# Queries and keys of chunks 0 and 1 as seven-product pairs, and the down stage of chunk 1 behind four gate/up tiles

## The chip, the cores and the metric

The kernel runs on one core of one Trainium2 chip. The metric is the device time of one execution in microseconds (us), median of several runs. The *granted clock* is the share of its full clock that TensorE was given. The span, from the first to the last instruction in the profile, is about 1.8 us shorter than the time. PE is TensorE, PEld its weight loads, DVE is VectorE, ACT is ScalarE, POOL is GpSimd, SP is SyncE, which only issues transfers here.

## The reference

```python
def reference(A_x, A_wqkv, A_wo, B_x, B_w_gate, B_w_up, B_w_down, gate_w):
    # x: 1 x 2048 x 1024 in bf16; 32 heads of 32; Df = 3584
    g = sigmoid((x * gate_w).sum(-1, keepdims=True))
    # a: local attention. Row s sees rows s, s-2, ..., s-14 (8 of them)
    qkv = (x @ wqkv).reshape(B, S, 3, H, Dh)
    logits = sum over Dh of q[s] * k[s - 2w], scaled, w = 0..7, masked below row 0
    a = (softmax(logits) weighted sum of v) @ wo
    # b: feed-forward on the same x
    b = (gelu(x @ w_gate) * (x @ w_up)) @ w_down
    return g * a + (1 - g) * b
```

(Shortened; the sums are written out in words.)

## The kernel before

The 2,048 rows are worked on in four chunks of 512. TensorE does the matrix products. VectorE does the attention: it multiplies queries by shifted keys, adds up, and later multiplies the weights by shifted values; each of these instructions covers 128 x 2,048 elements. Between the two steps the sums are turned over by transposing copies that SyncE issues, and the softmax runs on VectorE and ScalarE.

Many products are done two chunks at a time with seven products of half size in place of eight (Strassen's scheme in Winograd's form). That needs *forms*, sums and differences of the weights and of x, which VectorE makes ahead of the products, and afterwards additions, also on VectorE, from PSUM, the memory in whose banks the products land. Before the change, queries and keys of chunks 0 and 1 were computed plainly; the values, the second half's projections, gate/up and down were pairs already.

A list scheduler inside the program decides the order in which instructions are put down on each engine. It runs when the program is built, from its own estimates. On the chip the order is fixed: an engine whose next instruction must wait, waits, whatever stands behind it (6.11 us in an example below).

```python
    def main():                      # the order of TensorE's work (cut)
        # ... all 32 transposes of chunk 0's rows ...
        yield from qkv_outer(0)      # queries of chunk 0, plainly
        yield from qkv(0, 1)         # keys of chunk 0, plainly
        yield from gate(0)
        yield from qkv_pair(0, [2])  # values of chunks 0 and 1 as a pair
        yield from gate_sum(0)
        yield from qkv(1, 0)         # queries and keys of chunk 1, plainly
        yield from qkv(1, 1)
        yield from gate(1)
        yield from halo(1)
        for sup in range(NSUP):
            c0 = 2 * sup
            more = sup + 1 < NSUP
            parts = down(c0)
            yield from ffn(sup, parts, [gate_sum(1)] if sup == 0 else [])
            yield from parts[2]
            if more:
                yield from halo(c0 + 2)
                yield from gate(c0 + 2)
                yield from gate(c0 + 3)
                yield from qkv_pair(c0 + 2)      # "the second stage" below
                # ...
            for part in down(c0 + 1):            # down stage of chunk 1
                yield from part

    def gate(c):                     # (cut)
        i, free = bank_take()        # a PSUM bank
        # ... eight small matmuls into the bank ...
        zt = work.tile([P, SC], F32, tag="u2", bufs=2, name="zt")   # shares its two buffers with the u2 copies
        e = dve(0.63, lambda: nc.vector.transpose(out=zt[:], in_=banks[i][:]), [o])
        yield e
        bank_give(i, e)              # the bank is free when VectorE has read it
        e = dve(0.1, lambda: nc.vector.tensor_copy(out=zq[:], in_=...zt...), [e])
```

## Time and profile before

| | before |
|---|---|
| time, median of 3 runs | 725.7 us (725.52 to 726.15) |
| first gate/up product | 88.11 us |
| gates 2 and 3 begin | 312.65 us |
| second query/key/value stage ends | 387.26 us |
| last matmul ends | 720.08 us |

The prediction shows how busy the engines are. One stage that it does not cut out is needed later. This is its row in the table by stage (stretch, length, then busy time and count of PE, PEld, DVE, ACT, POOL, the granted clock, DMA share, GB/s), for the gates and projections of chunks 2 and 3:

```profile
312.65:387.26 74.61, 73.74 (x363) 44.38 (x369) 66.66 (x123) 37.58 (x66) 0.54 (x1) 1.00 0.39 115
```

The stage is 74.61 us long and PE is busy for 73.74 of them; DVE has 66.66 us of work and so 8 us of room.

### The profile page before, as it was taken

The numbers are of one execution on the slowest core, as the hardware profiler recorded it, in microseconds if no ns is written. First come the engines' busy times: TensorE is split into PE (matmuls) and PEld (weight loads), VectorE is DVE, ScalarE is ACT, GpSimd is POOL, SyncE is SP. The second block draws the span as 40 slices with busy tenths as digits, with TensorE's granted clock in tenths as the row PEclk, the third lists the DMA queues.
The fourth block names the chain that finished last, engine by engine and source line by source line (L and its number), as shares of the span: only waits on it lengthen the run. The fifth ranks groups of instructions, "written<-read, shape, count | busy, mean of one in ns | idle before, by whom it ended". The sixth has DMA issues, their size and how long they took to land.

```text
span 723.8 us, 9915 instructions
## 1 busy us (share of the span) xinstructions
PE 713.6 (99%) x3314; PEld 351.1 (49%) x3381; DVE 598.5 (83%) x898; ACT 315.3 (44%) x535; POOL 71.8 (10%) x128
## 2 busy tenths in 40 slices
PE   8999999999999999999999999999999999999997
PEld 5666644444444444455665444444444444444443
DVE  1799999999999899799599976999999995794200
ACT  2353465557655532035552114567558557110110
POOL 1000433343121100100000000000000000001000
PEclk9999999999999999999999999999999999999999
DMA  9944799989989979945239999786566657999992
GB/s 313 236 149 103 222 354 318 334 256 349 267 218 193 274 239 299 344 143 146 58 97 300 362 324 309 236 186 177 157 178 159 177 157 178 313 326 331 327 304 99
DMA packets 180931, 172.12 MB, mean 238 GB/s; under 512 B 56464, under 2 KB 137360, under 8 KB 180880
## 3 DMA queue, kind: packets, MB, share of 16 engines
q1 hardware_dynamic: 172048, 143.69, 68.5%
q0 software_dynamic: 8544, 27.27, 10.7%
q8 instruction: 26, 0.43, 0.2%
q10 hardware_dynamic: 288, 0.52, 0.2%
q14 instruction: 25, 0.20, 0.1%
HBM read 129.50 MB, written 28.31 MB: 218 GB/s over the span
## 4 chain that ended last, share of the span: by engine, by line
PE 83%; DVE 8%; DMA 4%; issue 4%; POOL 1%; ACT 0%; DVEq 0%; POOLq 0%; ACTq 0%
PE ps L995 35%; PE ps L1159 28%; PE ps L628 12%; PE ps L496 8%; DMA fforms<-ring 1%; DVE ring L457 1%; DVE ring L576 1%; DVE hT L1058 1%; DMA ring<-in_B_w_down_dram 1%; DMA ring<-in_A_wqkv_dram 1%; DMA hT<-in_A_wo_dram 1%; DMA hT<-in_B_w_down_dram 1%; DVE hT L1120 1%; DVE hT L1039 1%; DVE hT L433 0%
## 5 line engine op out<-in xcount | busy, mean ns | idle before, releaser
L995 PEld LDWEIGHTS <-ring 128*128 128x128 bf16 x1568 | 153.2, 98 | 185.8 <-issue 1.6
L995 PE MATMUL ps<-lend,ring 128*128 128x512 bf16 x877 | 210.5, 379 | 1.3 <-ACT m L1049 0.4
L995 PE MATMUL ps<-tf,ring 128*128 128x512 bf16 x659 | 162.6, 379 | 0.7
L1159 PE MATMUL ps<-ring,hT 128*128 128x512 bf16 x696 | 159.7, 379 | 0.6
L1159 PEld LDWEIGHTS <-hT 128*128 128x128 bf16 x708 | 69.2, 98 | 83.3
L945 DVE TENSOR_TENSOR xbuf<-xbuf,lend 128x2048 bf16<-128x2048 bf16 x64 | 77.4, 1215 | 7.5 <-DMA xbuf<-xbuf 7.5
L798 DVE TENSOR_TENSOR xbuf<-qo,lend 128x2048 bf16<-128x2048 bf16 x64 | 76.7, 1216 | 0.1
L804 DVE TENSOR_TENSOR xbuf<-xbuf 128x2048 bf16<-128x2048 bf16 x56 | 68.2, 1217 | 0.3
L628 PEld LDWEIGHTS <-ring 128*128 128x128 bf16 x384 | 49.3, 129 | 34.4 <-DVE lend L481 0.9
L1024 ACT COPY ps<-ps 128x512 f32<-128x512 f32 x56 | 32.0, 571 | 55.6 <-PE ps L995 55.5
L1067 ACT ACTIVATE gl<-ps 128x512 bf16<-128x512 f32 x56 | 33.5, 598 | 49.6 <-PE ps L995 48.5
L1194 ACT ACTIVATE ost<-ps,omg 128x512 bf16<-128x512 f32 x16 | 11.0, 688 | 100.6 <-PE ps L1159 81.9
L1186 POOL DMA_DIRECT2D out_dram<-ost x24 | 13.0, 540 | 411.0 <-ACT ost L1194 319.1
L1159 PE MATMUL ps<-ring,qo 128*128 128x512 bf16 x187 | 48.5, 379 | 0.2
L466 POOL DMA_DIRECT2D fforms<-ring x56 | 30.6, 546 | 175.3 <-DVE ring L457 166.1
L628 PE MATMUL ps<-lend,ring 128*128 128x512 bf16 x203 | 47.0, 380 | 0.7 <-DVE lend L481 0.5
L1039 DVE TENSOR_TENSOR hT<-hT,gl 128x1024 bf16<-128x1024 bf16 x56 | 38.3, 683 | 11.3 <-ACT hT L1036 11.3
L953 DVE TENSOR_TENSOR xbuf<-xbuf 128x1024 bf16<-128x1024 bf16 x64 | 42.0, 683 | 0.4
L1079 DVE TENSOR_TENSOR u<-ps,u 128x512 f32<-128x512 f32 x56 | 38.3, 684 | 4.6 <-PE ps L995 3.2
L628 PE MATMUL ps<-tf,ring 128*128 128x512 bf16 x173 | 40.1, 379 | 0.2
L1058 DVE TENSOR_TENSOR hT<-ps,m 128x512 bf16<-128x512 f32 x56 | 38.2, 683 | 1.5 <-PE ps L995 1.4
L1075 ACT COPY u<-ps 128x512 f32<-128x512 f32 x56 | 32.9, 587 | 15.1 <-PE ps L995 15.1
(110 smaller groups left out, 697.1 us busy)
## 6 DMA issues: line engine op xcount, KB each, us to landing
ring<-dforms SPq DMA_DIRECT2D x112, 256.0 KB, 5.3
ring<-in_B_w_down_dram SPq DMA_DIRECT2D x84, 256.0 KB, 4.6
ring<-in_B_w_gate_dram SPq DMA_DIRECT2D x56, 256.0 KB, 4.8
fforms<-ring POOLq DMA_DIRECT2D x56, 256.0 KB, 5.3
ring<-fforms SPq DMA_DIRECT2D x56, 256.0 KB, 4.0
ring<-in_B_w_up_dram SPq DMA_DIRECT2D x42, 256.0 KB, 4.7
ring<-in_A_wqkv_dram SPq DMA_DIRECT2D x32, 256.0 KB, 5.4
ring<-oforms SPq DMA_DIRECT2D x32, 256.0 KB, 5.7
```

Of the source, the lines that this page charges most:

```text
L496: nc.tensor.matmul(banks[bk][:], lhsT=lhsT, rhs=xT(c, kt), start=(kt == 0), stop=(kt == KT - 1))
L628: nc.tensor.matmul(banks[bk][:], lhsT=lhsT, rhs=rhs[:, kt, :], start=(start and kt == 0), stop=(kt == KH - 1), skip_group_check=True)
L798: V(out=w3(box[t]), in0=q_b, in1=k_w, op=ALU.mult)
L804: V(out=w3(box[0]), in0=w3(box[0]), in1=w3(box[t]), op=ALU.add)
L945: return dve(tt(n), taking(("p", t), lambda: V(out=w3(box["p", t]), in0=w3(box["ab"]), in1=v_w, op=ALU.mult)), [("qkv", c, 2, t), abo] + ( ...
L953: V(out=s4(t)[:, t % 2], in0=w3(box["p", t])[:, 0:4], in1=w3(box["p", t])[:, 4:8], op=ALU.add)
L995: nc.tensor.matmul(banks[bk][:], lhsT=wv[:, k, fl * P:(fl + 1) * P], rhs=rhs[:, k, :], start=(start and k == 0), stop=(k == KH - 1), skip_ ...
L1039: yield dve(tt(2 * SC), lambda f=f: nc.vector.tensor_tensor(out=hrow[:, f, :], in0=hrow[:, f, :], in1=gl[f][:], op=ALU.mult), [e, ev[f, "g ...
L1058: ev[f, "up2"] = dve(tt(SC, True), lambda f=f: nc.vector.tensor_tensor(out=hs(f, 1), in0=v3(banks[Bk[f]][:]), in1=v3(m5[f][:]), op=ALU.add ...
L1067: nc.scalar.activation(out=gl[f][:, SC:2 * SC], in_=banks[A[f]][:], func=ACT.Gelu_apprx_tanh)
L1079: e = dve(tt(SC, True), lambda f=f: nc.vector.tensor_tensor(out=u2[f][:], in0=banks[Dk[f]][:], in1=u2[f][:], op=ALU.add), [o, ev[f, "u2"]])
L1159: nc.tensor.matmul(banks[bk][:], lhsT=l, rhs=wv[:, i, :], start=(start and k == 0), stop=(q == last and i == 1), skip_group_check=True)
```

## The change

The intent: 32 matmuls fewer. Queries and keys of chunks 0 and 1 become pairs, like the values. The first of the seven products needs chunk 0 alone, so it is put at the front while chunk 1 is still on its way. Chunk 1's attention now starts later, so its down stage goes behind the first four gate/up tiles of the second half; that in turn needs chunk 3's queries, keys and values to be parked in DRAM for a while. Double-width forms, fewer and wider window sums, and new constants of the scheduler come with it.

```diff
     def main():
-        # 32 transposes, then
-        yield from qkv_outer(0)
-        yield from qkv(0, 1)
-        yield from gate(0)
+        yield from turn_rows()           # the first 16 transposes
+        yield from qkv_pair(0, [0])      # first_pair: chunk 0's products, 16 transposes, gates 0 and 1, the rest
+        yield from qkv_pair(0, [1])
+        yield from gate_sum(0)
+        yield from gate_sum(1)
         yield from qkv_pair(0, [2])
-        yield from gate_sum(0)
-        yield from qkv(1, 0)
-        yield from qkv(1, 1)
-        yield from gate(1)
         yield from halo(1)
...
+        yield from qkv_pair(2)
+        parts = down(1)
+        yield from ffn(1, 0, NE, parts)  # NE = 4: four gate/up tiles, then chunk 1's down stage
+        yield from parts[2]
+        parts = down(2)
+        yield from ffn(1, NE, FT, parts)
...
+    def park(which):                     # chunk 3's projections wait in DRAM
+        return Op("POOL", ..., lambda: nc.gpsimd.dma_start(out=parked[which]..., in_=hrow[:, r:r + NT, 0:SC]), ...)
...
-    w.run([(0.0, main()), (0.0, loads()), (0.0, late_x()), (0.88, wforms()), ..., (1.43, qkv_forms()), (1.3, preps()), (0.13, attention()), (0.36, scores())])
+    w.run([(0.0, main()), (0.0, loads()), (0.0, late_x()), (0.0, moves(3)), (0.71, wforms()), ..., (2.67, qkv_forms()), (2.06, preps()), (0.06, attention()), (0.34, scores())])
```

## The prediction

> **What bounds the kernel now.** I read four views in this order: the page's first line, the table of busy time by stage, the head of the timeline, and the chain of waits together with who waited for whom. The page says that TensorE (PE) has hardly any idle time, and VectorE (DVE) is second:
>
> ```profile
> span 723.8 us, 9915 instructions
> PE 713.6 (99%) x3314; PEld 351.1 (49%) x3381; DVE 598.5 (83%) x898; ACT 315.3 (44%) x535; POOL 71.8 (10%) x128
> ```
>
> A busy PE need not be a PE at its rate, so the next step is the rate. In the chain of waits (start, duration, what), whole stretches look like this:
>
> ```profile
> 9.82 10.74 PE ps L496 x49
> ...
> 189.53 10.74 PE ps L995 x49
> 200.32 10.74 PE ps L995 x49
> ...
> 692.29 10.74 PE ps L1159 x49
> ```
>
> Between two of these starts lie 10.79 us and 50 matmuls (one record in fifty is missing), so a 512-column matmul costs 10.79/50 = 0.2158 us, the same in the projections (L496), in gate/up (L995) and in the down stage (L1159). The program before has 3,280 of them apart from the warm-up: 3,280 x 0.2158 = 707.8 us. Add the four gate products (8 packed matmuls each, 0.55 us by the chain, 2.2 us in all). The first of the 3,280 starts at 7.02 us and the last ends at 720.1 us; of those 713.1 us, 3.1 us are left for the small gate sums and for all waits of PE. The stage table agrees (columns: stretch, length, then busy time and count of PE, PEld, DVE, ACT, POOL, clock, DMA share, GB/s):
>
> ```profile
> 0.00:7.02 7.02, 5.01 (x37) 3.21 (x38) 2.10 (x7) 3.22 (x6) 2.61 (x12) 1.00 0.70 194
> 7.02:88.11 81.09, 80.67 (x384) 51.60 (x391) 63.59 (x97) 30.59 (x53) 8.27 (x13) 1.00 0.70 204
> 88.11:256.00 167.89, 166.58 (x770) 75.81 (x783) 163.61 (x245) 98.99 (x174) 47.95 (x80) 1.00 0.96 285
> 256.00:321.00 65.00, 64.44 (x305) 29.92 (x309) 57.87 (x89) 16.97 (x28) 4.32 (x8) 1.00 0.87 273
> 321.00:390.00 69.00, 68.38 (x326) 41.28 (x334) 60.95 (x115) 33.07 (x58) 0.00 (x0) 1.00 0.40 115
> ```
>
> PE is full in every stage, DVE is also full from 88 to 256 us (163.61 of 167.89), and DMA is half idle around 321 to 390. The whole recoverable time of PE is therefore the 7.02 us ahead of the first product, the end after 720.1 us, and some 2 us inside. The largest waits inside are these:
>
> ```profile
> PE ps L628 <- DVE lend L481: 0.5, 1, 0.5
> PE ps L995 <- ACT m L1049: 0.4, 1, 0.4
> PE ps L496 <- DVE lend L1259: 0.3, 1, 0.3
> ```
>
> **What the Trainium skill says.** "TensorE: Matmul & The Clock Gate", section "Wait — 56ns, not 53.3ns?", gives a warm start-to-start spacing of N/2.4 GHz plus about 2.5 ns, 215.7 ns for 512 columns; the trace has 215.8. So matmuls cannot get cheaper here, only fewer. "Perfetto Trace Analysis", section "Identifying the Most-Contended Engine", warns that matmul busy time is no measure of closeness to the roofline; that is why I count matmuls by spacing instead of trusting the 99%. "VectorE: DVE Perf Modes", section "The perf-mode tier table", has a bf16 tensor_tensor of 2,048 elements at 1,224 ns and tensor_tensor with a PSUM operand at one element a cycle; the trace has 1,215 ns for the first and 684 ns for the 512-column additions from PSUM, and successive ones start 1.14 and 0.60 us apart. "DMA: Bandwidth & Descriptors", section "Why small descriptors are slow (HBM only)", speaks of a fixed cost per packet; the before kernel fetches the gate vector two bytes at a time, and while that transfer is in flight (6.5 us to landing, issued at 1.34) the DMA falls to 134 GB/s between 5 and 7 us from 355 before and 389 after. That fits, but another cause is possible.
>
> **The change, part by part.** (1) *Queries and keys of chunks 0 and 1 as pairs.* Computed plainly they take 4 x 64 = 256 matmuls (L496). A pair takes seven products of 4 matmuls for each of 4 tiles, 112 instead of 128, so 224 for both. That is 32 fewer; the order of the built programs confirms it, 3,248 against 3,280, and gate/up (1,568), down (1,008) and the later projections are unchanged. Gain on PE: 32 x 0.2158 = 6.9 us, all of it on the path that sets the end, as PE never rests.
>
> (2) *The head.* The 32 row transposes stay (16 + 16 rather than all 32 first). Before, they run from 4.04 us, when the first x tile lands, to 6.6, at 0.079 us apiece:
>
> ```profile
> 4.04 2.52 PEld L1252 LDWEIGHTS <-hT 128*128 128x128 bf16 x32 [1.43 <-DMA hT<-in_A_x_dram]
> 5.87 1.56 ACT L1257 COPY lend<-ps 128x512 bf16<-128x512 bf16 x3 [0.18 <-PE ps L1252]
> ...
> 7.02 5.34 PE L496 MATMUL ps<-lend,hT 128*128 128x512 bf16 x23 [0.29 <-DVE lend L1259]
> ```
>
> After, the first half of x (512 KB in two queues) should land at about the same 4.0 us; 16 transposes (1.3 us), and the last evacuation (0.59 us on ACT) and its waits, put the first product near 6.2 us. But 16 more transposes (1.3 us) now stand inside the product stream, so its effective start is 7.5 us against 7.02: a loss of 0.4 to 0.5, not a gain. "Chunk 0's own products at the front" are the 32 matmuls that need no second chunk. They end near 7.5 + 6.9 = 14.4 us. Then the first form of chunk 1's rows is wanted, hence chunk 1's transposing loads. 1 MB of x and 2 MB of query weights lie ahead of them at 390 GB/s: about 10 us. A 512 KB transposing load ran at 200 GB/s later in the trace (57.0 to 59.5 us), 2.6 us each, so with about 1 us to land the halves come at 13.5 and 16 us; the form is one 1.2 us DVE operation, ready near 14.8. Loss about 0.4 us. The second form (16 + 1.2 + 0.6 = 17.8) is wanted only after the gates and four more products (19.3): no wait. Head in all: +0.8 us.
>
> (3) *DVE.* Added: forms for two more projections, and 16 additions from PSUM (16 x 0.60 = 9.6 us). All forms now work on double width (0.60 instead of 2 x 0.333 us), so the three first-stage projections take 24 x 0.60 = 14.4 us instead of 5.3, and the second-stage ones save 1.6. Four casts go (-2.7) and 64 window sums become 32 of double width (-2.3). Sum about +12 us of 598. What matters is where: summing spacings over the built order up to gate/up tile 0's final multiply gives 76 us before and 82 after, while PE gets there at 100.9 us before and some 6 us earlier after. 82 us of work into 95, of which the first 10 have no data: full, but just fitting. Over the following 27 tiles the sums are 156 and 157 us against 27 x 28 x 0.2158 = 163 us on PE: no worse than before.
>
> (4) *Chunk 1's down stage behind 4 tiles.* It neither adds nor removes a matmul. It gives chunk 1's attention, which starts later now, 112 x 0.2158 = 24 us more before the 252 down products need it. Between gate/up 0's last multiply and gate/up 1's first, DVE has 117 us of work against some 133 us on PE. The price is three 1 MB parkings in DRAM and back plus a 512 KB move, instead of 2 MB of moves. Parking falls into the stage with DMA share 0.40. A second pipeline filling at tile 4 may cost some 0.2 us; the 0.5 us wait on L481 may go as its operation moves ahead. I set these against each other: 0.
>
> (5) *Twelve more PSUM copies on ACT*, 7 us in a stage where ACT is busy 30.59 of 81.09: hidden. The end is untouched (the last 3.6 us are one copy and the store).
>
> **Sum.** 725.7 - 6.9 + 0.8 + 0 = 719.6 us, 0.8% less.
>
> **Rivals.** *A large gain, over 2%*: the deadlines that the diff gives its scheduler move from 88.5 to 82.0 and from 308 to 297, so one may think that 11 us go by then. Against it: 14.5 us would be needed, while removing 6.9 us of products and every wait of PE still leaves 3,248 x 0.2158 + 2.2 + 7.02 + 3.7 plus the 1.9 us between span and time = 715.7, and the head is not shortened. This gives 716. *The head stalls*: transposing loads of 512 columns may be slower than those of the attention, or queue behind the key weights; each us of lateness beyond 16 us is soon a us lost. This gives 721 to 724. *DVE becomes the bound at the first gate/up tiles*, as it enters them full: the additions then come late, PE waits at L1140's products, 720 to 724; against it, the order was built from spacings that match the trace. *The parked copies or the 512 KB move come late*, while the down stage draws 340 GB/s: PE waits at tile 4, +1 to +3 us; against it, the move has the last 72 down products (15.5 us) and a tile to finish.
>
> **Range and chances.** The floor of 716 bounds it below; stalls have no such bound but the order of work is tuned. Eight in ten: 717.2 to 723.0. Over 2% faster means below about 711.2, under the floor: 1%. Over 2% slower needs 740, 20 us of new waits: 2%. Within 2%: 97%.
>
> **What would show it.** Right: still 10.79 us per 50 matmuls, 3,248 of them; first query product at 6 to 6.5 us; PE idle below 1 us between 13 and 18 us; the first gate/up product near 82 (88.11 before); DVE over 95% busy from 45 to 240 us; last matmul near 714. Wrong: PE waiting on a transposing load, or on DVE forms or additions (L713, L1207, L1228), for more than 2 us in all; or a first gate/up product below 80.

## More of the kernel before

The next view is SyncE's queue (start, time for issuing, instruction), where the attention of chunk 1's first half shows:

```profile
248.79 1.36 SPq L867 DMA_TRANSPOSE xbuf<-xbuf  x1
283.38 1.47 SPq L936 DMA_TRANSPOSE xbuf<-xbuf  x1
...
292.87 1.32 SPq L936 DMA_TRANSPOSE xbuf<-xbuf  x1
...
298.87 1.17 SPq L328 DMA_DIRECT2D ring<-in_A_wqkv_dram  x2
```

L867 is the transposing copy of the summed products, L936 the two copies that bring the weights back, L328 the loads of the second stage's weights. The attention's three copies are issued before the weights are, so the two do not meet.

## The result, and the profile after

The changed kernel took 727.5 us (median of 4 runs, 726.76 to 729.78) against 725.92 us of the kernel before on the same chip (725.52 to 726.5). The ratio is 1.0026, with a 95% interval of 1.0002 to 1.005. The class, within 2%, was predicted; the 719.6 us and the range of 717.2 to 723.0 were missed.

The profile taken with the result happened to be the slowest of the four runs (span 728.0 us). So I ran the changed kernel twice more, unchanged, as a yardstick: e0_after and e0b_after.

> The changed kernel again, untouched, as the base of this batch and to see whether its profiled run (729.8 us, the slowest of four) was typical. If its waits are fixed by the order of its instructions: 727 to 728 us, and a profile that again loses about 5 to 7 us of PE between 309 and 350 us and has the first gate/up product near 85 us. If they were an accident of that one execution (for example a PE that was still at the slow clock at 4 to 9 us), the profile has the first gate/up product below 84 us and less than 4 us lost in the second query/key/value stage.

e0_after: 726.96 us (726.34 to 727.59), ratio 1.0018, 1.0003 to 1.0033.

> The changed kernel unchanged, beside the two: 726.7 to 727.6, its second stage 78 to 82 us, as before.

e0b_after: 727.56 us (727.35 to 729.02), ratio 1.0032, 1.002 to 1.0045. Its second stage (the gates and the pairs) took 79.6 us.

The page of e0_after:

```profile
span 724.6 us, 9937 instructions
...
PE 714.2 (99%) x3353; PEld 344.5 (48%) x3353; DVE 610.1 (84%) x862; ACT 325.2 (45%) x549; POOL 74.0 (10%) x130
```

DVE rose from 598.5 to 610.1 us, as predicted. The matmul's rate has not changed either. In the chain of waits of the changed kernel, 50 matmuls again take 10.79 us:

```profile
434.79 10.74 PE ps L1309 x49
445.58 6.50 PE ps L1309 x30
```

The table by stage of e0_after, with the same columns as before (the first stretch begins with the first query product, the last but one is that of gates 2 and 3 and the second pairs; chunk 0's down stage is left out):

```profile
6.84:85.47 78.63, 77.50 (x386) 45.57 (x386) 67.37 (x92) 34.11 (x60) 8.14 (x12) 1.00 0.64 201
85.47:252.30 166.83, 166.78 (x773) 75.53 (x772) 165.50 (x256) 104.07 (x180) 48.75 (x80) 1.00 0.91 280
...
309.38:388.03 78.65, 74.88 (x370) 44.33 (x369) 70.74 (x103) 37.52 (x66) 2.26 (x3) 1.00 0.51 138
388.03:724.60 336.57, 333.10 (x1549) 150.58 (x1540) 259.04 (x349) 135.03 (x223) 9.54 (x17) 1.00 0.82 250
```

Set against the same stages before: up to the first gate/up product 85.47 us instead of 88.11 (-2.64); gate/up of the first half 166.83 instead of 167.46 (-0.63); chunk 0's down stage the same 57.08; gates and second pairs 78.65 instead of 74.61 (+4.04); the rest up to the last matmul 333.13 instead of 332.82 (+0.31). The sum is +1.08 us, and the last matmul ends at 721.16 instead of 720.08. So two things went wrong: the head gained 2.64 us instead of 6.1, and a stage that has the same products in both kernels got 4 us longer. In that stage PE is busy for 74.88 us of 78.65; before, it was busy for 73.74 of 74.61.

The view of waits shows whom PE waited for in that stage, in e0_after (what waited, what it waited for, us in total, times, longest):

```profile
PE ps L776 <- ACT u2q L824: 1.3, 2, 1.1
PE ps L776 <- DVE qo L841: 1.2, 2, 0.6
PE ps L776 <- DVE ring L713: 1.0, 1, 1.0
PE ps L776 <- DVE lend L841: 0.3, 1, 0.3
```

and its first line in the slowest run, the one profiled first, where the stage took 81.83 us:

```profile
PE ps L776 <- DVE ring L713: 3.2, 2, 2.3
```

Before, PE waited for DVE for 0.5 us there, and for nothing else. The listed waits thus come to 3.8 us against 0.5, which is 3.3 of the 4.04 us; the rest is not put down to a wait by the view. The slow run shows how it comes about. SyncE's queue and then VectorE's timeline (start, duration, instruction, and in brackets how long the engine stood idle and for what):

```profile
298.49 0.81 SPq L354 DMA_DIRECT2D ring<-in_A_wqkv_dram  x2
299.61 4.62 SPq L1079 DMA_TRANSPOSE xbuf<-xbuf  x2
304.32 3.38 SPq L354 DMA_DIRECT2D ring<-in_A_wqkv_dram  x7
```

```profile
308.38 1.23 DVE L1088 TENSOR_TENSOR xbuf<-xbuf,lend 128x2048 bf16<-128x2048 bf16 x1 [6.11 <-DMA xbuf<-xbuf]
311.64 0.70 DVE L713 TENSOR_TENSOR ring<-ring 128x1024 bf16<-128x1024 bf16 x1 [2.03 <-DMA ring<-in_A_wqkv_dram]
```

The two transposing copies of chunk 1's weights (L1079) stand behind only two of the loads of the second stage's weights; the other loads are issued 6 us later. VectorE stood still for 6.11 us until the copy had landed. The forms of the second stage (L713) stood behind that wait, and PE waited for forms for 3.2 us in all. In e0_after the copies were issued from 297.23 us on, 2.4 us earlier, and VectorE could go on 7.6 us after the first issue instead of 8.8; it stood still for 2.4 us, and soon after for 2.7 us until the weights for a form had landed (2.0 us in the slowest run), and PE lost 1.0 us to forms. The Trainium skill, "PSUM — Partial Sum Buffer", section "Engine vs sequencer instructions", says that the queues of ScalarE, VectorE and GpSimd are strict FIFO. The trace agrees: for 6.11 us VectorE did nothing, and nothing behind that instruction was started.

One more comparison of timelines goes with the meeting (whether it is its reason, a_early0 tests below): the first multiplication of queries by keys starts at 43.6 us instead of 32.7 us, and chunk 1's first half has its last one at 256.0 us instead of 238.8 us. The copies that were at 248.79, 283.38 and 292.87 us are now at 273.81 us and from 297.23 us.

### The profile page after: what moved, and what is told of

Same layout as the page of the kernel before. It is cut to its first block, busy times and chain, and to the rows that moved or that the text cites. A ratio compares the mean times of both kernels' runs of the same rounds, so it can differ in the third digit from the quotient of the medians. Undisturbed runs are those within 1.5% of the kernel's fastest.

```text
span 728.0 us, 9871 instructions
## 1 busy us (share of the span) xinstructions
PE 711.1 (98%) x3287; PEld 344.0 (47%) x3353; DVE 610.0 (84%) x862; ACT 325.2 (45%) x549; POOL 73.8 (10%) x130
## 3 DMA queue, kind: packets, MB, share of 16 engines
q0 software_dynamic: 9328, 30.42, 11.8%
## 4 chain that ended last, share of the span: by engine, by line
PE 47%; DVE 5%; DMA 2%; issue 1%; SPq 0%; ACT 0%; DVEq 0%
PE ps L1140 22%; PE ps L1309 20%; PE ps L776 5%; DVE xbuf L1088 2%; DMA xbuf<-xbuf 2%; DVE ring L713 1%; DMA ring<-dforms 1%; DVE xbuf L1098 1%; SPq L1079 0%; DVE xbuf L1102 0%; DVE qo L851 0%; DVE qo L841 0%; DVE zt L884 0%; DVE xbuf L947 0%; DVE lend L518 0%
## 5 line engine op out<-in xcount | busy, mean ns | idle before, releaser
L1140 PEld LDWEIGHTS <-ring 128*128 128x128 bf16 x1568 | 153.1, 98 | 186.2 <-issue 1.8
L1140 PE MATMUL ps<-lend,ring 128*128 128x512 bf16 x879 | 211.1, 379 | 1.4 <-ACT m L1198 0.4
L1140 PE MATMUL ps<-tf,ring 128*128 128x512 bf16 x658 | 162.9, 380 | 0.7
L776 PEld LDWEIGHTS <-ring 128*128 128x128 bf16 x544 | 69.1, 128 | 57.5 <-issue 6.5
L1088 DVE TENSOR_TENSOR xbuf<-xbuf,lend 128x2048 bf16<-128x2048 bf16 x64 | 77.6, 1217 | 11.2 <-DMA xbuf<-xbuf 11.0
L941 DVE TENSOR_TENSOR xbuf<-qo,lend 128x2048 bf16<-128x2048 bf16 x64 | 77.1, 1217 | 2.6 <-ACT lend L834 2.6
L947 DVE TENSOR_TENSOR xbuf<-xbuf 128x2048 bf16<-128x2048 bf16 x56 | 68.2, 1217 | 0.2
L776 PE MATMUL ps<-lend,ring 128*128 128x512 bf16 x279 | 64.8, 380 | 2.3 <-ACT u2q L824 1.4
L776 PE MATMUL ps<-tf,ring 128*128 128x512 bf16 x253 | 59.1, 380 | 5.8 <-DVE ring L713 3.2
L1189 DVE TENSOR_TENSOR hT<-hT,gl 128x1024 bf16<-128x1024 bf16 x56 | 38.2, 683 | 8.4 <-ACT hT L1182 8.3
L1232 ACT ACTIVATE gl<-u 128x512 bf16<-128x512 f32 x56 | 35.4, 632 | 13.6 <-DVE u L1228 13.4
L1228 DVE TENSOR_TENSOR u<-ps,u 128x512 f32<-128x512 f32 x56 | 38.2, 683 | 2.1 <-PE ps L1140 1.3
L1098 DVE TENSOR_TENSOR xbuf<-xbuf 128x2048 bf16<-128x2048 bf16 x32 | 38.9, 1217 | 0.1
## 6 DMA issues: line engine op xcount, KB each, us to landing
ring<-dforms SPq DMA_DIRECT2D x112, 256.0 KB, 5.1
ring<-in_B_w_down_dram SPq DMA_DIRECT2D x84, 256.0 KB, 5.2
ring<-in_B_w_gate_dram SPq DMA_DIRECT2D x56, 256.0 KB, 5.6
fforms<-ring POOLq DMA_DIRECT2D x56, 256.0 KB, 4.9
ring<-fforms SPq DMA_DIRECT2D x56, 256.0 KB, 4.2
ring<-in_B_w_up_dram SPq DMA_DIRECT2D x42, 256.0 KB, 5.5
ring<-in_A_wqkv_dram SPq DMA_DIRECT2D x32, 256.0 KB, 4.2
ring<-oforms SPq DMA_DIRECT2D x32, 256.0 KB, 5.7
```

The lines of the kernel that those rows point to most:

```text
L776: nc.tensor.matmul(banks[bk][:], lhsT=lhsT, rhs=rhs[:, kt, :], start=(start and kt == 0), stop=(kt == KH - 1), skip_group_check=True)
L941: V(out=w3(box[t]), in0=q_b, in1=k_w, op=ALU.mult)
L947: V(out=w3(box[0]), in0=w3(box[0]), in1=w3(box[t]), op=ALU.add)
L1088: return dve(tt(n), taking(("p", t), lambda: V(out=w3(box["p", t]), in0=w3(box["ab"]), in1=v_w, op=ALU.mult)), [("qkv", c, 2, t), abo] + ( ...
L1098: V(out=p0.rearrange("p (u n) -> p u n", u=2), in0=lo, in1=hi, op=ALU.add)
L1140: nc.tensor.matmul(banks[bk][:], lhsT=wv[:, k, fl * P:(fl + 1) * P], rhs=rhs[:, k, :], start=(start and k == 0), stop=(k == KH - 1), skip_ ...
```

## The experiments

Eighteen kernels ran, two of them the unchanged one. Where a run is compared by stage, "the stage" is gates 2 and 3 with the second pairs. "Head" is all up to the first gate/up product. The first theory, B for backlog: the change makes VectorE's work before chunk 1's attention more and later than it can make up for, and the rest falls into the stage. The rivals: it is only the order on the queues; it is the parking; and, for the head, the loads are issued too late. (The parking is in every one of the changed kernels; no run takes it out.)

### The copies behind the loads (e1_tail)

```diff
-   tail=4.0 if h == 0 else 1.1
+   tail=4.0 if h == 0 else 6.0 if h == 2 else 1.1
```

The scheduler is told that chunk 1's copies land later, so it puts them behind eight weight loads instead of two, and the forms ahead of the products with the values. (VectorE's order changes with it from 281 us on, other attention work included, so this is not the queue order alone.)

> Only the scheduler's guess of how long the two transposes back of chunk 1's first attention half take to land is raised by 4.9 us (its tail from 1.1 to 6.0). PE's order does not change, all orders are the same up to about 276 us; behind that the transposes stand after 8 query-weight loads on SP instead of after 2, and DVE gets the weight forms before the first product with the transposed weights. Queue theory (SP issues the weights late and DVE is parked in front of a transfer): PE loses less than 2 us in the second query/key/value stage, 722 to 724 us. Backlog theory (DVE simply has too much work by then, the order only moves the wait): within 1 us of the changed kernel, with as much PE lost there or a few us later.

725.9 us (725.42 to 726.48), ratio 1.0004, 0.9989 to 1.0018; the stage took 77.8 us. About 1 us came back of 4. That is as much as the stage differs between two runs of one kernel (78.7 and 79.6 us), and the two intervals of the ratio, this one and e0_after's, overlap. The queue order is at most a small part of the cause; that it is one is not shown.

### The products with the values later still (e3_pv3)

```diff
+   pv operation: bias=3.0 if h == 2 else None
```

> Only DVE's order is changed in the second query/key/value stage: the products of chunk 1's first attention half with the values get a bias of 3 us in the scheduler, so that the weight forms come before them. SP's order up to there stays: the two transposes still stand behind 2 query-weight loads and ahead of the other 22. If DVE's being parked before the transfer is what costs: 3 to 5 us gained, 722.5 to 724.5 us. If the late issue of the weights is what costs: at most 1.5 us gained, with PE waiting on forms that wait on the weights' DMA. Backlog theory: no gain.

733.25 us, ratio 1.0097, 1.0081 to 1.0114. The stage fell to 76.25 us, and the wait came back, larger, in chunk 1's down stage, whose products with the output weights need that attention. In 386 to 620 us:

```profile
PE ps L1309 <- DVE qo L1106: 5.4, 2, 3.7
```

What was pushed out of the stage was work that has to be done by a fixed point. It did not vanish. A part of the loss is the clock's: from within the wait of 3.7 us on, the granted clock was 0.50 for 6.8 us.

### Chunk 1's down stage back in its place (e2_down_early)

```diff
-   NE = 4
+   NE = 0        # and the 512 KB move goes with it
```

> The second half of the change undone: chunk 1's down stage stands directly behind the second query/key/value stage again (no early gate/up tiles, no 512 KB move; the parking in DRAM stays). Backlog theory: chunk 1's attention is now wanted 24 us earlier, while DVE's work is 12 us more than before, so PE waits at the down stage: 732 to 745 us. If the reordering is not needed or itself costs time: 725 to 728 us, no new wait of PE at L1309's counterpart.

733.13 us, ratio 1.0104, 1.0089 to 1.012. The stage was as long as with the move (78.8 us), and the time after it was 6.7 us longer than in e0_after (339.8 us against 333.1 us to the last matmul). So the move of the down stage is worth some 6 us within the changed kernel, and the stage's loss does not come from it: VectorE's order is the same as e0_after's up to 395 us. The time came out as the backlog theory said, but not where it said: PE did not wait in the down stage at all. It waited in the gate/up tiles behind it, for ScalarE's copies, 2.7 us (L1195) and 1.0 us (L1169), and after the longer wait the clock was 0.50 for 3.4 us.

### Three mends of the head at once (h12m_head)

```diff
+   gates 0, 1: ScalarE copies the bank to SBUF, VectorE transposes from there
+   gate(0) goes behind the first pair
+   x and the query weights in fewer, larger loads; gate row by GpSimd
```

> The changed kernel with the head mended in three places: ScalarE empties the gates' PSUM banks, the gate of chunk 0 goes behind the first pair, and the loads of x and of the query weights are fewer and larger, so that the two transposing loads of chunk 1 do not queue behind them. Theory H (the head loses its 3.2 us to the transposing loads that are issued late and to banks that wait for VectorE): the first gate/up product starts at 82.3 to 84.0 instead of 85.4. For the whole time the theories differ. Backlog theory (VectorE is the bound from about 45 us to the down stage of chunk 1): an earlier gate/up stage does not make chunk 1's attention earlier by as much, the second query/key/value stage loses what the head gained, and the time is 725 to 727. Rival (the second stage's loss is a matter of its own, of queue order and parking): the gain is kept, 723.5 to 725.

731.51 us, ratio 1.0084, 1.005 to 1.0119; the first gate/up product came at 85.78 us. Both expectations failed. The bank waits were gone, as meant, but the first form's products began at 18.32 us instead of 17.10: 27 of chunk 0's own matmuls took 6.96 us instead of 6.17, and the second form started only 0.5 us earlier than in e0_after, although the two transposing loads were issued from 3.29 us on instead of 8.86. But in this execution the granted clock was 0.50 from 9.03 to 12.44 us, in the middle of those products, so its head does not tell what the loads did. The run's mean clock was 0.993; the one run of four at 0.999 took 729.93 us, still 3 us more than e0_after's median. The greater part of the loss came later: the scheduler, given other operations at the front, put what follows in another order. From the first gate/up product to the gates of chunks 2 and 3 it lost 1.3 us against e0_after, in the stage 1.5 (with one wait of 3.1 us for a form, and 6.8 us at half the clock from within it on), and in the last stretch of gate/up 3.2 (146.0 us instead of 142.8; one wait of 3.1 us). A change at the front that reorders the rest cannot be read as a change at the front.

### Twelve microseconds less for VectorE, in the same order (d_less)

```diff
-   V(out=b11, in0=b12, in1=b11, op=ALU.subtract)
+   V(out=b11[:, :, 0:192], in0=b12[:, :, 0:192], in1=b11[:, :, 0:192], op=ALU.subtract)    # and the other three
```

> The changed kernel, wrong on purpose: the 36 subtractions for the down stage's forms work on 192 of 512 columns, which takes about 12 us from VectorE (36 times 0.686 less 0.353), four fifths of it before 170 us; no order changes on any engine. Backlog theory: chunk 1's attention is some 8 to 12 us earlier, the stage of gates 2 and 3 and the second query/key/value pairs takes under 76 us instead of 78.7, the time is 722 to 724. Rival (that stage loses its 4 us to the queue order, the copies to DRAM and their landing, whatever VectorE does before): it stays at 78 to 79 us and the time at 726 to 727.

726.87 us (wrong result, on purpose), ratio 1.0019; the stage took 79.1 us. Theory B, as I had put it, failed: 12 us of VectorE's time given back (summed over the 36 instructions) changed nothing. The reason is in the timeline: from 231 to 301 us VectorE's instructions in this run stand within 0.1 us of those of e0_after. Between attention instructions stand multiplications of the gate/up tiles that wait for PE, so VectorE cannot run ahead of PE within a fixed order. Time that falls free in front of such a wait is spent in it: in front of the multiplications of queries by keys (L941 in e0_after), of the tiles' multiplications (L1189) and of their additions (L1207, L1228) VectorE stood idle for 24.3 us instead of 13.4.

### Twelve microseconds more, in both kernels (d_more, b_more)

```diff
-   f0: V(out=b11, in0=b12, in1=b11, op=ALU.subtract)
+   f0: the same, three times       # b12-(b12-(b12-b11)) is the same result
```

> The changed kernel with 18 more subtractions of 0.686 us on VectorE (12.3 us; three times the same subtraction gives the same result up to rounding), no order changed. Backlog theory: VectorE has no room left, most of the 12 us reaches the end: 732 to 738. Rival (VectorE fits, as predicted, with room of some us): under 729.

> The kernel before with the same 12.3 us more on VectorE. If the kernel before had room on VectorE, and the change spent it, this costs less here than in the changed kernel: 726.5 to 730. If the kernel before was already at VectorE's bound in this stretch, it costs as much as there: 732 or more.

d_more: 738.33 us, ratio 1.0174; b_more: 739.85 us, ratio 1.019 (1.0173 to 1.0207, so unclear by the 2% rule), that is 14.2 us over the kernel before for 12.3 us of work. Some of this is the clock: b_more's three other runs are listed at 0.998 and took 2.5 to 2.9 us longer than the profiled one at 1.0. The profiled runs, both at 1.0, took 10.5 us more than e0_after's (d_more, on another chip) and 11.8 us more than that of the kernel before (b_more). In both, the first half's gate/up stage took it: 176.3 us instead of 166.8 us after, 179.6 us instead of 167.5 us before. PE waited there, in d_more and in b_more:

```profile
PE ps L1140 <- ACT m L1198: 5.8, 8, 1.2
```

```profile
PE ps L995 <- ACT m L1049: 8.2, 5, 2.7
```

(L1198 and L1049 are ScalarE's copies of a product into the two m5 buffers; a buffer is free when VectorE's addition has read it.) So the prediction's "full, but just fitting" holds for this stage in both kernels: of 12.3 more microseconds at most two fit (1.8 in d_more, 0.5 in b_more, by the profiled runs). And the change has not spent a reserve here, for the kernel before had hardly any.

### Empty the gates' banks with ScalarE (f1_bank_tail)

```diff
+   zs = work.tile(..., tag="gl") for chunks 0 and 1
+   o = act(0.5, lambda: nc.scalar.copy(out=zs, in_=banks[i][:]), [o]); bank_give(i, o)
    e = dve(0.63, lambda: nc.vector.transpose(out=zt[:], in_=zs), [o])
```

On top of e1_tail. (The text says that no order on VectorE changes. That was not quite so: four small shifts came among the first 33 instructions; from there on the order is the same.)

> The run e1_tail plus one thing: ScalarE copies the two first gates' PSUM banks to SBUF and frees them, VectorE transposes from the copy. No order on VectorE changes. Bank theory (the third and fourth first-form products wait for banks that stand behind VectorE's queue): the wait of TensorE for the stream transposes (1.3 us) goes, the first gate/up product starts at 84.0 to 84.6 instead of 85.3, the time is 724.6 to 725.3. Rival (another wait takes its place at once, the forms of VectorE or ScalarE's copies): the first gate/up product stays at 85.2 to 85.5 and the time at 725.7 to 726.2.

725.26 us (724.23 to 725.94), ratio 0.9992, 0.9978 to 1.0006; the first gate/up product came at 84.73 us instead of 85.30. In the head of the changed kernel (e0b_after, 14 to 90 us), PE waits for VectorE's reading of the gates' banks, and its weight loads wait for the query weights (4 to 14 us):

```profile
PE ps L776 <- DVE zt L884: 1.3, 2, 1.0
```

```profile
PEld L590 <- DMA hT<-in_A_wqkv_dram: 2.6, 3, 1.2
```

In f1_bank_tail the wait for the bank is gone, but another one is in its place:

```profile
PE ps L776 <- ACT u2q L658: 0.8, 1, 0.8
```

(In e1_tail itself the wait for the bank is 0.7 us.) The 0.57 us by which gate/up begins earlier is a gain of the edit. The first form's products themselves began 0.7 us earlier in this execution (16.27 us instead of 16.98), but that alone moves nothing: in seven profiles whose order is the same up to there (after, e0_after, e0b_after, e1_tail, e2_down_early, e3_pv3, p_short) they began between 16.15 and 17.10 us, and the first gate/up product came between 85.23 and 85.47 us all the same. The earlier PE comes, the longer it waits for the bank (1.3 us in e0b_after, which began at 16.34 us; 0.7 in e0_after, at 17.10); in p_nowait, at 18.22 us, it did not wait for it at all. VectorE sets the time there. So the bank theory holds, and the rival in part: the new wait of 0.8 us took more than half of what the old one gave. The time, 725.26 us, is in the range of the bank theory, but its interval overlaps with e1_tail's. The new wait is for the u2 copy of ScalarE, and f2_zt and f3_zt_gl, below, deal with such waits.

### Take away the landing, and take away the work (p_nowait, p_short)

```diff
    # p_nowait, h == 2 (chunk 1's first half)
-   in0=w3(box["ab"]), in1=v_w
+   in0=v_w, in1=v_w
    # p_short, h == 2: the same operands, an eighth of the columns
```

> The changed kernel, wrong on purpose: the eight products with the values of chunk 1's first half read the value window twice instead of the transposed weights, so VectorE does not stand still until that transposing copy has landed; same number and size of instructions, same order. Theory P (VectorE parked on the late landing keeps the forms of the second query/key/value stage back): the stage of gates 2 and 3 and the pairs takes 75 to 76.5 us instead of 78.7, time 724 to 725.5. Rival (the stage loses its 4 us to the amount of attention work that now lies in it, or to the weights' own landing): 77.8 or more, time over 726.3.

> The changed kernel, wrong on purpose: the same eight products work on an eighth of their columns, about 8 us less for VectorE inside the second query/key/value stage, and still wait for the landing; no order changes. If the amount of work in the stage is the cause: stage 74.5 to 76.5 us, time 723 to 725. If it is the landing (of the transposing copy or of the weights): 77.5 or more, time over 726.

p_nowait: 727.4 us, ratio 1.0029, stage 79.6 us. It told nothing: the first product's target is a buffer that the transposing copy still reads, so VectorE waited for the copy all the same (2.30 us). (Its head, too, had 3.4 us at half the clock, from 8.86 us on.)

p_short: 725.01 us, ratio 0.999, 0.9976 to 1.0003, stage 76.7 us. VectorE waited for the landing even longer (3.6 us), and yet the stage was 2 us shorter than in e0_after (2.9 us shorter than in e0b_after); it and the time just miss the expected ranges of 74.5 to 76.5 and 723 to 725 us, and do not reach those of the landing theory (77.5 or more, over 726). Two of PE's waits:

```profile
PE ps L776 <- ACT u2q L824: 1.4, 2, 1.1
...
PE ps L776 <- DVE ring L713: 0.2, 1, 0.2
```

The waits for the additions L841 on the queries (1.2 us) are gone, and those for forms are down from 1.0 to 0.2 us. So about half of the loss, 2 us, is the attention's own work crossing the forms and additions. Another part, 1.4 us of u2q, has nothing to do with this work.

### The shared buffer (f2_zt, f2b_zt, f3_zt_gl)

The wait for u2q is explained by three lines of e0_after:

```profile
317.64 0.17 DVE L888 COPY zq<-zt 128x16 f32<-128x16 f32 x1
...
317.91 0.59 ACT L824 COPY u2q<-ps 128x512 f32<-128x512 f32 x1 [3.21 <-DVE zq L888]
...
318.55 1.02 PE L776 MATMUL ps<-lend,ring 128*128 128x512 bf16 x4 [1.07 <-ACT u2q L824]
```

Before the change, the first u2q copy starts 4.6 us after the stage's first pair product (318.25 and 313.63 us), as soon as its product is done. Here that would be 315.0 us; but ScalarE stood idle for 3.21 us, until VectorE had copied zq out of zt. zt and u2 share two buffers, and zt came late, because VectorE was late: it was written at 316.43 us although the gates' products were done at 310.4 us. In the kernel before, VectorE read the first bank at 313.94 us, 1.3 us after the gates had begun, and the buffers were free in time.

```diff
-   zt = work.tile([P, SC], F32, tag="u2", bufs=2, name="zt")
+   zt = work.tile([P, 2 * SC], BF16, tag="gl", bufs=3, name="zt")[:].bitcast(F32)    # chunks 2 and 3
```

> The run f1_bank_tail plus one thing: the transposed gate of chunks 2 and 3 gets a buffer of its own kind instead of one of the two that ScalarE's u2 copies use. If the 1.3 us that TensorE waits for the u2q copies are the shared buffer's (ScalarE waits for the copy zq out of it), they go: the second stage takes 76.5 to 77 us instead of 78.1 and the time is 724.0 to 724.8. If VectorE's lateness only shows in the next wait (the additions L841, the forms): the stage stays over 77.6 and the time at 725 to 725.6.

> f2_zt unchanged, a second time: 723.8 to 724.6 if the first result was no chance; 725 or more if it was.

> The run f2_zt plus one thing: the transposed gate of chunk 0 leaves the shared u2 buffers too. If the head's wait for the u2q copy (0.8 us in f1_bank_tail) was the same shared buffer, no wait for u2q is left before the first gate/up product, which starts 67.4 us or less after the first first-form product; time 723.4 to 724.3. If not, such a wait is seen again in some of the runs: 724.2 to 725.

f2_zt: 724.23 us (723.17 to 727.02), ratio 0.9985, 0.9966 to 1.0003; the stage took 76.7 us instead of 78.1 in f1_bank_tail. No wait for u2q was left; VectorE's order is the same in both, so the shared buffer is shown to be the reason of that wait. How much of the stage it is worth is less sure: in the repeat the stage took 77.7 us, only 0.4 less than in f1_bank_tail, because PE waited 1.8 us instead of 0.8 for an addition (L841), and in time the step from f1_bank_tail to f2_zt lies within the intervals. f2b_zt, the same kernel again on another chip: 724.5 us (724.39 to 724.86), ratio 0.9987, 0.9974 to 0.9999, beside the changed kernel's 727.56 us in the same rounds. f3_zt_gl, with chunk 0's zt moved as well: 725.07 us (723.57 to 725.78), ratio 0.9991, 0.9977 to 1.0005. It has no u2q wait in the head either: gate/up begins 67.7 us after the first form's first product, against 68.1 in f2b_zt (which waited 0.5 us for u2q) and 68.4 and 68.9 in the two runs of the changed kernel. (f2_zt had no such wait and took 67.4.) The first gate/up product came at 83.95 us, 0.5 us before f2b_zt's; but the time is not better, and both numbers for that case (67.4 us or less, 723.4 to 724.3 us) were missed. The two longest waits in f2b_zt's stage:

```profile
PE ps L776 <- DVE qo L841: 1.8, 1, 1.8
PE ps L776 <- DVE lend L841: 0.9, 1, 0.9
```

In f2_zt the gates began at 308.86 us and the wait for L841 on the queries was 0.8 us; in f2b_zt it was 308.40 and 1.8; in f3_zt_gl 307.86 and 1.5. The stage ended at 385.55, 386.06 and 385.46 us. What the head gains, the stage takes back; as I read it, since its end hangs on VectorE and on the landings there. This much of theory B stands, though no run tests it alone.

### Only the order of VectorE in the stage (g_fm6)

```diff
+   weight forms of the second pairs: bias=-0.6
```

> The run f2_zt with the weight forms of the second query/key/value stage moved ahead of attention work by up to three places on VectorE, nothing else told to the scheduler. If the order of VectorE in the stage is what remains (forms 0.6 us, additions 1.7 us), the stage takes 75 to 76.5 us and the time is 723.3 to 724.3. If the same work only changes places: within 0.5 us of f2_zt.

728.32 us, ratio 1.0035, 1.0019 to 1.0052; the stage took 81.0 us. This is a miss, and one of the wrong sign: 4 us slower than f2_zt. PE waited once for a form, 3.6 us, and VectorE stood 2.0 us in front of one until its weights had landed. The profiled run is also the slowest of six (730.73), and its head was 2 us longer than f2_zt's with the same order there, and the clock was 0.50 for 3.4 us in the stage, right after the wait for the form; so the size of this miss is uncertain, not its sign.

### Start the attention early, or make it smaller with the scheduler knowing (a_early0, dl_224)

```diff
    # a_early0, scores of chunk 0's first half: q times q, no keys needed
-   in1=k_w, deps [("qkv", c, 0, t), ("qkv", c, 1, t)]
+   in1=q_b, deps [("qkv", c, 0, t)]
    # dl_224: as d_less with 224 columns, and the cost that the scheduler sees is made smaller with it
-   t = tt(n * NW)
+   t = tt(n * CUT)
```

> The changed kernel, wrong on purpose: the scores of chunk 0's first half multiply the queries by themselves, so they need no keys and can start at about 30 us instead of 43.6; VectorE's work is the same and the scheduler knows of it. If the late start is why chunk 1's attention lies in the second stage, its first half's scores end at 248 us or before (256 now), the stage takes 74.5 to 77 us, the time is 723 to 725.3. If it is the amount of work, and the start is made up for on the way: scores end at 252 us or later, stage 77.5 to 79, time 725.8 to 727.5.

> The changed kernel, wrong on purpose: the 36 subtractions for the down stage on 224 of 512 columns, about 10.8 us less for VectorE as in d_less, but now the scheduler knows it, so the attention moves forward in the order. If the amount of work before the stage is the cause: scores of chunk 1's first half end at 249 us or before and its products with the values lie for the most part before the pairs, the second stage takes 74.5 to 76.8 us instead of 78.7. If not: 77.5 or more. The time is told less surely (the order after it changes too): 724 to 729.

a_early0: 732.12 us, ratio 1.0092, stage 79.0 us. (Meant to be wrong, it passed the comparison with the reference; so little do the scores of 256 of 2,048 rows weigh there.) The scores began at 35.2 us and those of the first half ended at 52.4 instead of 68.3 us. By the second half the lead was 11 us (170.2 against 181.5 us), and by chunk 1's first half there was none (258.8 against 256.0 us). The gate/up stage took 4.4 us more; PE waited there for an addition, 3.0 us at once, and from the end of that wait on the clock was 0.50 for 3.4 us. In the stage PE waited 4.2 us for forms, against 1.0 in e0_after, so its time went in another way there. So the late start of the attention, which I had read off the timeline as the reason, is not by itself what puts it into the stage.

dl_224: 733.08 us, ratio 1.0099, stage 75.8 us. With 10.8 us less work that the scheduler knows of, chunk 1's first half had its last score multiplication at 247.8 us, and the stage lost only 1.2 us more than before. But the gate/up stage grew from 166.8 to 173.6 us, where PE waited most (L1199 is the line L1198 of the other kernels):

```profile
PE ps L1141 <- ACT m L1199: 3.5, 3, 1.9
```

The stage's loss is therefore tied to how much of chunk 1's attention is left for it, which agrees with theory B. That the load decides this, and not the order, is not shown: the order changed too, and a gate/up stage that is 6.8 us longer gives the attention more time as well. And in this kernel a lighter load in a new order is no gain: the new order puts attention ahead of tile work, and gate/up pays. The time missed its range (724 to 729 us). How much of that is this one order, and how much any order would pay, stays open; I ran no other.

### In one table

| run | time, us | ratio to before | gate/up begins | the stage, us |
|---|---|---|---|---|
| kernel before (profile of its own) | 725.7 | 1 | 88.11 | 74.6 |
| e0_after, e0b_after | 726.96, 727.56 | 1.0018, 1.0032 | 85.47, 85.28 | 78.7, 79.6 |
| e1_tail | 725.9 | 1.0004 | 85.30 | 77.8 |
| e2_down_early | 733.13 | 1.0104 | 85.46 | 78.8 |
| e3_pv3 | 733.25 | 1.0097 | 85.23 | 76.3 |
| h12m_head | 731.51 | 1.0084 | 85.78 | 80.2 |
| d_less | 726.87 | 1.0019 | 85.40 | 79.1 |
| d_more | 738.33 | 1.0174 | 85.58 | 79.4 |
| b_more (on the kernel before) | 739.85 | 1.019 | 88.11 | 74.1 |
| f1_bank_tail | 725.26 | 0.9992 | 84.73 | 78.1 |
| p_nowait | 727.4 | 1.0029 | 85.72 | 79.6 |
| p_short | 725.01 | 0.999 | 85.32 | 76.7 |
| f2_zt, f2b_zt | 724.23, 724.5 | 0.9985, 0.9987 | 84.72, 84.49 | 76.7, 77.7 |
| f3_zt_gl | 725.07 | 0.9991 | 83.95 | 77.6 |
| g_fm6 | 728.32 | 1.0035 | 86.69 | 81.0 |
| a_early0 | 732.12 | 1.0092 | 85.32 | 79.0 |
| dl_224 | 733.08 | 1.0099 | 85.24 | 75.8 |

Stage times are from one profiled run each and move by about 1 us between runs of one kernel (78.7 and 79.6; 76.7 and 77.7), and by 3 us in the slowest (81.8). The parking was never taken out, but dl_224 and e3_pv3 have it and stages of 75.8 and 76.3 us, so hardly more than 1.2 of the 4.0 us could be its.

**Half the clock.** In e0_after the granted clock is 1.0 from 9.91 us, where its record begins, to 723.30 us. Six other profiles have a stretch at half of it in mid-run. Two of them (the clock is the third figure from the end), from e3_pv3 and from the head of h12m_head:

```profile
420.72:427.55 6.83, 4.63 (x11) 1.64 (x12) 6.83 (x10) 1.29 (x3) 0.00 (x0) 0.50 0.09 33
```

```profile
9.03:12.44 3.41, 3.41 (x21) 2.38 (x20) 1.96 (x4) 0.64 (x2) 0.00 (x0) 0.50 1.15 318
```

The others are a_early0 (from 195.1 us), e2_down_early (457.6), g_fm6 (339.6) and p_nowait (8.9) with 3.4 us each; h12m_head has a second one of 6.8 us from 316.2 us. All but the two in the head began during a long wait of PE or within 0.5 us of its end: 3.7 us in e3_pv3, 3.6 in g_fm6, 3.1 in h12m_head, 3.0 in a_early0, 2.7 in e2_down_early. Three waits of that length had none behind them (3.1 us in h12m_head and in a_early0, 2.7 in b_more), so the length alone does not decide it; what does stays open. Products in such a stretch start 0.43 us apart instead of 0.216, so by estimate half of PE's busy time in it is lost, besides the wait: 1.7 us for a stretch of 3.4. The losses of these five runs are in part the clock's, and so are two stage times: by the same estimate some 1.7 of g_fm6's 81.0 us and 3.0 of h12m_head's 80.2 (PE was busy for 3.41 and 6.00 us in them).

## Why the prediction was wrong

The predicted last matmul was near 714 us; in e0_after it ended at 721.2. The 7.2 us between them are 3.5 in the head, 4.0 in the second query/key/value stage, -0.6 in the first gate/up stage and +0.3 in the rest.

**Right.** The rate of the matmul, and with it the gain of 6.9 us for 32 products; 12 us more for VectorE (11.6 measured); ScalarE's extra copies did no visible harm in total (ScalarE is busy for 45% of the span, 44% before). "Full, but just fitting" was right for gate/up of the first half: it took no longer than before, and 12 us more did not fit in.

**Step 2, the head: "+0.8 us" was 4.1 to 4.3.** The sentence that failed is "The second form ... is wanted only after the gates and four more products (19.3): no wait." I had asked when the form is ready, and not what stands behind it on VectorE. In e0b_after the third and fourth product of the first form had no PSUM bank, since the banks of the two gates are freed by VectorE's transposes, and those stood in VectorE's queue behind the second form and the weight forms: 1.3 us. That this is what sets the head is shown twice: an earlier start of PE moves nothing while the bank is not freed (the seven profiles under f1_bank_tail), and with the bank and the shared buffer both freed f3_zt_gl, which starts as early (16.24 us against 16.34), has its first gate/up product at 83.95 us instead of 85.28. These are 1.3 of the 3.3 us by which 85.28 exceeds the 82.0 that the prediction implied. Of the others, 1.5 us is the late start of the first form's products, at 16.34 us instead of some 14.8, and for 0.5 us no wait accounts. The late start is only argued: chunk 0's own products ended at 15.9 us instead of 14.4, after PE's weight loads had waited 2.6 us for the query weights. In e0_after they waited 1.3 us and the products ended at 16.6, since PE still ran at half its rate until 9.9 us (matmuls 0.43 us apart). That the query weights are late because of the queue of loads ahead of them is not shown; the one attempt to shorten that queue, h12m_head, fell into a stretch at half the clock.

**Step 4: "I set these against each other: 0" was 4.0, and 7.2 in the slowest run.** The prediction weighed only the price of the move. It never went through the second query/key/value stage, which has the same 336 products before and after. The profile of before had the hint, 8 us of room for VectorE in a stage of 74.61. Chunk 1's attention moved into it. Of the 4.0 us in e0_after, 1.3 are ScalarE waiting for a buffer shared with the late gate transposes (f2_zt: 1.4 us back, 0.4 in its repeat), and about 2 are attention work ahead of forms and additions (p_short: 2 us back); the remaining 0.7 us stays open. What the slowest run adds follows the transposing copies, which were issued 2.4 us later and let VectorE go on 1.2 us later still, so that VectorE idled 6.1 us instead of 2.4; as p_nowait failed to take that wait away, this size is read and not tested.

**The rivals.** "The head stalls" named the place and half of the size, but not the cause: in e0b_after the first form was ready at 15.5 us, before PE was through with chunk 0's own products (15.9), and the second at 17.5 us, so that PE waited for no transposing load. (The 200 GB/s that the prediction gives for such a load were measured on the attention's transposing copy, L867, which was in flight from 55.9 to 60.2 us.) "DVE becomes the bound at the first gate/up tiles" was not; it named the right engine and additions, but they came late 220 us further on. The late parked copies did not show either: in e0_after PE is busy for 333.10 of the last 333.13 us. No rival looked at the stage between, that of gates 2 and 3.

## What to carry to other kernels

When a change adds work to an engine that is full in a long stage (VectorE here: 165.50 of 166.83 us), ask at which later stage the delayed work comes out, and walk through that stage by its waits, even where its own products are unchanged. In engines with fixed order, look for buffers and banks that two streams share: what frees them may stand behind a wait that has nothing to do with them, and moving such a buffer is the cheap mend (here a bank, a buffer and the place of two copies in a queue made 727.56 into 724.5 us, which is 0.13% better than before). An experiment that lightens an engine's work shows nothing if the order is kept and the engine keeps pace with another one, and shows too much if the scheduler reorders everything. And read the granted clock of each stage before a loss is explained: in five runs here a wait of PE of 2.7 to 3.7 us went together with 3.4 or 6.8 us at half the clock.

## What the Trainium skill lacked or had wrong

- "TensorE: Matmul & The Clock Gate", section "Back-to-back issue gap", gives a sustained 131 ns per 512-column matmul in a stream of weight loads and matmuls, and calls N/2.4 + 2.5 ns the isolated gap only. In every run here such a stream goes at 10.79 us for 50, 215.8 ns each, and never faster over a stretch: the formula is the sustained rate here, as the section that the prediction cites has it.
- No page gives the time to landing of a transposing copy from SBUF to SBUF beside other loads; what the pages have on transposes are rates. For the 256 KB copies of the attention weights it was 3.8 to 9.0 us in three profiles of the changed order (median 5.7 to 5.8); the spread is as large as the loss that was looked for.
- "PSUM — Partial Sum Buffer", section "Engine vs sequencer instructions", states the strict FIFO, but not what it costs a tuned kernel: 12.3 us of extra instructions cost 10.5 and 11.8 us (profiled runs at the full clock) in two kernels with VectorE at 83 and 84% of the span, and 12 us less brought nothing.
